# A listed order for an attention phase, and the first expert chosen 384 tokens earlier

## The chip, the cores and the metric

One core of one Trainium2 chip. TensorE (PE; PEld is its weight load), VectorE (DVE), ScalarE (ACT), GpSimd (POOL) and SyncE (SP) each work through a list of instructions of their own, in order, and wait for each other by semaphores. The metric is the device time of one launch in microseconds. All data are float32 in HBM; matmuls run in float32, each as two instructions of the trace.

## What is computed

Two blocks follow each other. The first is a gated linear recurrence with complex gates per batch (4), head (8) and channel (48) over 768 time steps:

```python
for t in range(S):
    new_re = ar * S_re - ai * S_im          # gates, limited in magnitude
    new_im = ar * S_im + ai * S_re
    S_re, S_im = new_re + k[t] (x) v[t], new_im
    y[t] = q[t] @ S_re
```

Its output, laid out as 3072 tokens of 384 numbers, goes into a top-1 mixture of 8 experts:

```python
expert_idx = argmax(x @ w_gate)
gate_w     = softmax(x @ w_gate)[expert_idx]
out[mask]  = gate_w[mask] * (relu(x[mask] @ w1[e]) @ w2[e])     # 384 -> 1024 -> 384
```

## The kernel before

**Attention** is worked in chunks of 128 time steps, 6 to a batch, 24 in all. The gates become logarithms and angles, whose running sums (DVE scans) turn the recurrence into masked matmuls: within a chunk scores times values, between chunks a state of 96x48 per head.

- `front(u)` prepares one *unit* of 128, 256 or 384 time steps. There are ten: units 0 to 2 are batch 0, 3 and 4 batch 1, 5 and 6 batch 2, and 7 (384 steps), 8 (256) and 9 (128) batch 3. It loads gates and q, k (L335), runs logarithms, exponentials and sines on ACT with changes of the function table, scans (L357, L368) and elementwise work on DVE, and two multiplications per unit on POOL. It ends with four products on DVE into `zp` (L388) and ten DMAs on SP (L398, L401) that move `zp` into `hz0` or `hz1`, the layout in which PE reads it.
- `chunk(b, c)` is PE's part: transposed keys (L431), scores (L438), which DVE masks into `am` (L442), the state's and the values' share of the output (L450, L457), the new state (L465), and a transposing matmul (L473) whose result ACT copies into `xg` (L476). The logits come out of that same matmul.
- `route(b, r0, r1)` sorts tokens into experts: some 15 small DVE instructions, a count on PE (L514 to L519), and one indirect DMA per chunk on POOL (L533) that puts the rows into `xs_hbm`, 480 places for each expert. Batches 0 to 2 are routed whole, batch 3 after its chunks 2, 4 and 5. `cum` holds the places taken so far, `cumb` its bf16 copy for PE.
- `ranks()` (L540) runs once, when 2688 tokens are routed: it sorts the experts by their counts into `order`.
- `early_rows()` (L558) then lets SP read the number of the fullest expert from `order` (L256), load the two halves of its w1 (L573) and, once those 2688 tokens are in `xs_hbm`, its first 320 rows (`EARLY = 10` blocks of 32, L567), and its w2 (L575). w1 and w2 go into the two halves of `hz0`, which batch 3's first half has left.
- `early_layer()` (L582) is the first layer of that expert for those 320 rows, 24 matmuls on PE (L590), before the last tokens are routed.

**The experts** follow in turns, turn 0 being the fullest. `tokens(e)` loads rows (L736) and lets DVE transpose them (L260), `weights(e)` loads w1 and w2 (L726), then come the first layer (L767), the second (L786) and the scatter to the output (L707). Turn 0 has only its remaining 160 rows to load and to compute. The three w1 buffers are `hz0`, `hz1` and one of its own.

What sets the order: every step is entered into a `Plan` with an engine, a planned duration and the keys that it reads and writes. `Plan.order()` (L151) tries 144 priority rules in a list scheduling on these planned durations, and the steps are written to the engines in the order that comes out shortest. `P.PE` (L285) scales PE's planned durations. The expert phase has a second `Plan`, `M`.

Of the kernel before, what the change touches and what calls it, by code (L numbers as in the profile page):

```python
# [10 lines left out]
FP32 = mybir.dt.float32  # L11
BF16 = mybir.dt.bfloat16
I32 = mybir.dt.int32
# [7 lines left out]
C = S // 128  # L21
# [17 lines left out]
EARLY = 10  # L39
# [9 lines left out]
BIG = 1e9  # L49


class Plan:
# [27 lines left out]
    PE = 1.0, 1.0, 0.0  # L80
# [20 lines left out]
    def run(self, prio, edges, ins, back, stick):  # L101
# [10 lines left out]
        for _ in ops:  # L112
# [23 lines left out]
            free[eng] = issued = end = t + o["dur"] * (self.PE[t > self.PE[2] or back] if eng == "PE" else 1.0)  # L136
# [32 lines left out]
def gateloop_then_moe(ctx, tc, gates, qk, v, wg, w1, w2, out):  # L169
# [57 lines left out]
    key, above = const([128, E], "key"), const([128, E], "above")  # L227
# [3 lines left out]
    cum = const([128, E], "cum")  # L231
    cumb = const([128, E], "cumb", dt=BF16)
    nc.vector.tensor_scalar_mul(cum, base, 1.0 / 128)
    nc.vector.tensor_copy(cumb, cum)
# [9 lines left out]
    w1b, w2b = [z[:, 0:DT * F] for z in hz], [z[:, DT * F:2 * DT * F] for z in hz]  # L244
# [10 lines left out]
    def expert_of(e, eng):  # L255
        return ds(nc.values_load(order[0:1, TURNS[e]:TURNS[e] + 1], engines=(eng,), min_val=0, max_val=E - 1,  # L256
                                 skip_runtime_bounds_check_because="experts have numbers below E"), 1)
# [5 lines left out]
    with ExitStack() as att:  # L263
# [21 lines left out]
        P.PE = 1.8, 1.12, 60.0  # L285
# [192 lines left out]
        def route(b, r0, r1):  # L478
# [50 lines left out]
            dv(0.2, lambda: tt(cum, cum, ohs, ALU.add), ("ohs", "cum"), ("cum",))  # L529
            dv(0.2, lambda: nc.vector.tensor_copy(cumb, cum), ("cum",), ("cumb",))  # L530
# [8 lines left out]

        def ranks():  # L540
# [6 lines left out]
            dv(lambda: tt(key, cnt, keyb, ALU.subtract), ("RT",), ("key",))  # L547
            dv(lambda: tt(tmp, bc(key[:, None, :], full), bc(key[:, :, None], full), ALU.is_le), ("key",), ("tmp",))
# [9 lines left out]
        def early_rows():  # L558

            P.add("free", 0.0, lambda: None, (), tuple(("h", 0, c, h, part, d0) for c in range(3) for h in range(H) for part in range(2)  # L560
                                                       for d0 in (0, 32)) + ("hz0",))
            P.add("free", 0.0, lambda: None, (), (("A", 0), ("B", 0), "xb0"))
            P.add("free", 0.0, lambda: None, (), (("Q", 0), ("K", 0), "xrt0"))
            P.add("free", 0.0, lambda: None, (), tuple(("zp", part, x) for part in range(2) for x in range(2)) + ("ht0",))
            P.add("SP", 0.5, lambda: which.update({0: expert_of(0, mybir.EngineType.SP)}), ("order",), (("which", 0),))
            for i in range(4):
                last = P.add("SP", 0.65, lambda i=i: nc.sync.dma_start(  # L567
                    xb[0][32 * i:32 * i + 32, None, 0:EARLY, :], xv[:, which[0], 0:EARLY, 104 * i:104 * i + 96]),
                    (("which", 0), "xb0") + tuple(("rows", B - 1, c) for c in range(3)), (("xbA", i),), lat=2.0, wire=0.8)
# [389 lines left out]
```

## Time and profile before

| | us |
|---|---|
| three runs | 528.9, 529.66 (median), 532.79 |
| the profiled execution's own time | 530.8 |
| its span, first to last instruction | 529.0 |
| last transposing matmul of attention (L473) ends | 245.85 |
| first layer of the early rows (L590) | 249.17 to 265.4 |
| PE's last matmul ends | 522.8 |

| engine | busy us | share | instructions |
|---|---|---|---|
| PE | 450.7 | 85% | 2738 |
| DVE | 266.4 | 50% | 433 |
| ACT | 206.0 | 39% | 299 |
| POOL | 115.1 | 22% | 125 |

A share over the whole span hides that there are two phases. Until about 224 us DVE is the busy engine, with PE close behind from 60 us on; from 265 us on PE alone is. ACT loads its function table 25 times, 1283 ns each (L642).

### The profile page before, as it was taken

How to read it: one execution, taken by the hardware profiler on the slowest of the kernel's cores; microseconds unless marked ns; L12 is line 12 of the kernel's file. 1: busy time of each engine (PE TensorE's matmuls, PEld its weight loads, DVE VectorE, ACT ScalarE, POOL GpSimd, SP SyncE). 2: the span in 40 equal slices, each digit the busy share in tenths (PEclk: the TensorE clock that was granted, in tenths of full speed). 3: DMA queues.
4: the chain of work that ended last, by engine and by line, in shares of the span. 5: the costliest groups of instructions: out<-in, count | busy, mean ns of one | idle time of the engine just before them, and what ended most of it. 6: DMA issues, size and time to landing. Idle time of an engine off the chain costs nothing. (4 is left out here: it accounts for less than half of the span.)

```text
span 529.0 us, 7236 instructions
## 1 busy us (share of the span) xinstructions
PE 450.7 (85%) x2738; PEld 319.0 (60%) x2738; DVE 266.4 (50%) x433; ACT 206.0 (39%) x299; POOL 115.1 (22%) x125
## 2 busy tenths in 40 slices
PE   0055788898797398896999999999999999999995
PEld 0045677797697398885667554555555555555552
DVE  6899999999889899844001410122211111201101
ACT  6996887998595877442201000001000010010000
POOL 6174122142604621251000101010110202000012
PEclk9999789899979599998999999999999999999999
DMA  8577496786997974358597780304920451000001
GB/s 265 174 241 222 130 308 165 240 225 219 271 313 181 254 212 108 107 167 283 135 339 213 218 265 30 135 15 142 307 65 9 156 225 48 0 30 14 16 27 44
DMA packets 47945, 86.19 MB, mean 163 GB/s; under 512 B 21136, under 2 KB 36779, under 8 KB 45984
## 3 DMA queue, kind: packets, MB, share of 16 engines
q1 hardware_dynamic: 44064, 75.44, 47.9%
q0 software_dynamic: 3200, 9.86, 5.1%
q8 instruction: 23, 0.38, 0.3%
q10 hardware_dynamic: 640, 0.37, 0.3%
q14 instruction: 18, 0.15, 0.1%
HBM read 53.93 MB, written 13.24 MB: 127 GB/s over the span
## 5 line engine op out<-in xcount | busy, mean ns | idle before, releaser
L438 PE MATMUL bank<-hz 128*128 128x128 f32 x384 | 62.8, 321 | 42.9 <-DMA hz<-zp 31.1
L767 PE MATMUL bank<-Z,hz 128*128 128x416 f32 (+2 forms) x288 | 90.9, 468 | 0.0
L438 PEld LDWEIGHTS bank<-hz 128*128 128x128 f32 x384 | 56.1, 228 | 47.2 <-DVE cs L368 27.7
L707 POOL DMA_INDIRECT out_dram<-yo,gi x24 | 23.5, 977 | 243.2 <-DVE yo L718 229.5
L767 PEld LDWEIGHTS bank<-Z,hz 128*128 128x128 f32 x288 | 52.1, 190 | 35.4 <-issue 20.3
L773 ACT ACTIVATE ht<-bank 128x416 f32<-128x416 f32 (+2 forms) x20 | 10.1, 511 | 154.8 <-PE bank L767 154.8
L718 DVE TENSOR_SCALAR yo<-bank,gi 128x384 f32<-128x384 f32 x24 | 14.7, 616 | 92.5 <-PE bank L786 92.5
L786 PE MATMUL bank<-hz,ht 128*128 128x384 f32 (+1 forms) x176 | 59.5, 487 | 0.0
L182 DVE TENSOR_TENSOR zp<-Z,cs 128x1152 f32<-128x1152 f32 (+2 forms) x40 | 45.8, 1189 | 2.1 <-ACT cs L302 1.6
L786 PEld LDWEIGHTS bank<-hz,ht 128*128 128x128 f32 (+1 forms) x176 | 30.5, 175 | 19.9 <-issue 2.4
L770 DVE TENSOR_SCALAR ht<-bank 128x416 f32<-128x416 f32 (+2 forms) x20 | 11.6, 582 | 58.9 <-PE bank L767 58.9
L182 POOL TENSOR_TENSOR AB<-AB,C 128x1152 f32<-128x1152 f32 (+2 forms) x9 | 22.6, 2513 | 70.5 <-ACT C L302 64.6
L786 PE MATMUL bank<-w2b,ht 128*128 128x384 f32 (+1 forms) x128 | 37.5, 487 | 0.0
L786 PE MATMUL bank<-w2b,zp 128*128 128x384 f32 (+1 forms) x112 | 37.5, 486 | 0.0
L533 POOL DMA_INDIRECT xs_hbm<-xg,slot x24 | 27.2, 1134 | 42.7 <-DVE am L182 18.9
L767 PE MATMUL bank<-Z,w1b 128*128 128x448 f32 (+1 forms) x96 | 36.1, 517 | 0.0
L431 PE MATMUL bank<-ident,hz 96*128 96x96 f32 x160 | 22.4, 275 | 16.0 <-DMA hz<-zp 14.4
L465 PE MATMUL bank<-v,kt 128*96 128x48 f32 x320 | 31.9, 253 | 4.1 <-ACT kt L433 4.1
L773 ACT ACTIVATE zp<-bank 128x160 f32<-128x160 f32 (+2 forms) x12 | 5.2, 437 | 76.9 <-PE bank L767 62.0
L182 DVE TENSOR_TENSOR am<-bank,causal 128x512 f32<-128x512 f32 x48 | 31.7, 680 | 5.7 <-PE bank L438 3.9
L465 PEld LDWEIGHTS bank<-v,kt 128*96 128x96 f32 x320 | 30.3, 170 | 5.7 <-ACT kt L433 4.4
L182 POOL TENSOR_TENSOR Z<-Z,AB 128x1152 f32<-128x1152 f32 (+2 forms) x9 | 22.0, 2442 | 51.3 <-ACT AB L302 51.3
(135 smaller groups left out, 681.1 us busy)
## 6 DMA issues: line engine op xcount, KB each, us to landing
hz<-in_w_dram SPq DMA_DIRECT2D x9, 1536.0 KB
hz<-zp SPq DMA_DIRECT2D x24, 432.0 KB, 5.7
AB<-in_gates_dram SPq DMA_DIRECT2D x12, 576.0 KB, 3.8
Z<-in_qk_dram SPq DMA_DIRECT2D x12, 576.0 KB, 5.1
w2b<-in_w_dram SPq DMA_DIRECT2D x4, 1536.0 KB
v<-in_v_dram SPq DMA_DIRECT2D x8, 576.0 KB, 7.1
w1b<-in_w_dram SPq DMA_DIRECT2D x2, 1536.0 KB, 9.3
hz<-zp SPq DMA_DIRECT2D x8, 288.0 KB, 4.7
```

What stands on the lines that cost most here:

```text
L182: (eng or nc.vector).tensor_tensor(out=o, in0=a, in1=b, op=op)
L431: nc.tensor.transpose(KT[hf][:, (h % 4) * 96:(h % 4) * 96 + 96], hk[0:96, h], ident[0:96, 0:96])
L438: nc.tensor.matmul(SC[hf][:, (h % 4) * 128:(h % 4) * 128 + 128], lhsT=hk[:, h], rhs=hq[:, h], start=True, stop=True)
L465: nc.tensor.matmul(ST[0:96, h * D:h * D + D], lhsT=kt[par][:, h * 96:h * 96 + 96], rhs=V[:, cl, h * D:h * D + D], start=(c == 0 and h == 0 ...
L533: i = nc.gpsimd.indirect_dma_start(out=xs_hbm[:, :], out_offset=bass.IndirectOffsetOnAxis(ap=R[slot][:, c:c + 1], axis=0), in_=xg[:, (g0 + ...
L707: i = nc.gpsimd.indirect_dma_start(out=out[:, :], out_offset=bass.IndirectOffsetOnAxis(ap=index, axis=0), in_=y, in_offset=None, bounds_ch ...
L718: M.add("DVE", 0.62, lambda: nc.vector.tensor_scalar_mul(yo[yi], OB[ob][:, 0:DM], gate), (("O", ob),) + reads, (("yo", yi),))
L767: nc.tensor.matmul(HB[hb][:, 0:n - n0], lhsT=w1b[e % NW][:, c:c + 128], rhs=xrt[s][:, d, n0:n], start=(d == 0), stop=(d == DT - 1))
L770: M.add("DVE", 0.6, lambda f_=f_, hb=hb: nc.vector.tensor_scalar_max(ht[h][:, f_, n0:n], HB[hb][:, 0:n - n0], 0.0), (("H", hb),), (("ht", ...
L773: M.add("ACT", 0.6, lambda f_=f_, hb=hb: nc.scalar.activation(ht[h][:, f_, n0:n], HB[hb][:, 0:n - n0], func=ACT.Relu), (("H", hb),), (("ht ...
L786: nc.tensor.matmul(OB[ob][p0:p0 + m, 0:DM], lhsT=ht[t % NH][:, f_, c0:c0 + m], rhs=w2b[t % NV][:, f_ * DM:f_ * DM + DM], start=(f_ == 0), ...
```

## The change

1. **The order is listed.** `ORDER`, 989 numbers, says in which order attention's steps are written to the engines, in place of `P.order()`. The expert phase keeps its planner. The planner's model of PE's speed gets a third level, which no longer matters for attention's order.

```diff
+ORDER = [int(i) for i in (
+    "0 1 62 3 63 4 64 5 65 6 2 7 46 8 297 9 187 66 10 67 11 68 21 12 13 69 24 70 23 15 83 14 16 22 26 143 25 27 28 18 17 19 71 20 142 72 30 29 34 31 33 32 "
...
+).split()]
-        P.PE = 1.8, 1.12, 60.0
+        P.PE = (0.0, 1.8), (60.0, 1.12), (180.0, 0.95)
-            for i in P.order():
+            assert sorted(ORDER) == list(range(len(P.ops)))
+            for i in ORDER:
```

2. **The first expert is chosen at 2304 tokens**, when batch 2 is routed, by a function of its own. `ranks()` stays at 2688 tokens for the other seven; it puts the chosen one in front by adding `far`.

```diff
+        def fullest():
+            cnt = bank[2][:, 440:440 + E]
+            P.add("PE", 0.3, lambda: nc.tensor.matmul(cnt, lhsT=ones_b, rhs=cumb, start=True, stop=True), ("cumb",), ("RT",))
...
+            dv(lambda: tt(key, cnt, keyb, ALU.subtract), ("RT",), ("key",))
+            dv(lambda: nc.vector.tensor_reduce(top, key, axis=AX, op=ALU.max), ("key",), ("top",))
+            dv(lambda: nc.vector.scalar_tensor_tensor(out=above, in0=key, scalar=top, in1=e_f, op0=ALU.is_equal, op1=ALU.mult), ("top",), ("above",))
...
+                    nc.vector.tensor_reduce(first, above, axis=AX, op=ALU.add)
...
+            dv(lambda: nc.vector.tensor_scalar(out=far, in0=key, scalar1=top, scalar2=FAR, op0=ALU.is_equal, op1=ALU.mult), ("top", "key"), ("far",))
         def ranks():
...
+            dv(lambda: tt(key, key, far, ALU.add), ("far",), ("key",))
```

3. **The early rows** are 288 (`EARLY = 9`), they are loaded once batch 2's tokens are in `xs_hbm`, and w1 is loaded in one DMA into a buffer of its own, `w1first`, which needs no space that attention uses. w2 still goes into `hz0`. The three w1 buffers of the expert phase become `w1first`, `hz0`, `hz1`, and the one that the expert phase had of its own is gone.

```diff
-EARLY = 10
+EARLY = 9
-    w1b, w2b = [z[:, 0:DT * F] for z in hz], [z[:, DT * F:2 * DT * F] for z in hz]
+    w1b, w2b = [keep.tile([128, DT * F], FP32, name="w1first")] + [z[:, 0:DT * F] for z in hz], [z[:, DT * F:2 * DT * F] for z in hz]
-            P.add("SP", 0.5, lambda: which.update({0: expert_of(0, mybir.EngineType.SP)}), ("order",), (("which", 0),))
+            P.add("SP", 0.5, lambda: which.update({0: expert_of(0, mybir.EngineType.SP)}), ("first",), (("which", 0),))
...
-                    (("which", 0), "xb0") + tuple(("rows", B - 1, c) for c in range(3)), (("xbA", i),), lat=2.0, wire=0.8)
+                    (("which", 0), "xb0") + tuple(("rows", B - 2, c) for c in range(C)), (("xbA", i),), lat=2.0, wire=0.8)
+            P.add("SP", 0.65, lambda: nc.sync.dma_start(w1b[0][:, None, :], w1v[:, which[0], :]), (("which", 0),), (("w1", 0),), lat=1.9, wire=5.2)
...
-                bk, key = ((bank[7], "ones"), (bank[3], ("KT", 1)), (bank[5], "ST"))[f_ % 3]
+                bk, key = ((bank[7], "ones"), (bank[3], ("KT", 1)), (bank[5], "ST"))[(0, 0, 0, 1, 2, 0, 1, 2)[f_]]
...
-        w1b += buf("w1b", NW - 2, [128, DT * F])
```

4. **The places taken** are summed in bf16 directly: `cum` and its six casts into `cumb` (L530) are gone.

```diff
-            dv(0.2, lambda: tt(cum, cum, ohs, ALU.add), ("ohs", "cum"), ("cum",))
-            dv(0.2, lambda: nc.vector.tensor_copy(cumb, cum), ("cum",), ("cumb",))
+            dv(0.2, lambda: tt(cumb, cumb, ohs, ALU.add), ("ohs",), ("cumb",))
```

Where the listed order puts things, by the engines' lists of the built program. ACT still loads its table 25 times. On DVE, 16 instructions that stood ahead of unit 6's last product now stand behind it: four masks of batch 2, one scan of unit 7 and 11 small ones of batch 1's routing. Seven of unit 5's (six scans and an L355) now stand ahead of unit 4's last product; ahead of the last products of units 7, 8 and 9 stands almost the same as before. On PE, one transposing matmul (L473) more stands behind the first use of unit 7. The early layer's 24 matmuls are still PE's last of the phase, behind the last transposing matmul, and the last routing count stands behind six of them rather than three. On SP, reading `first`, loading w1 and loading w2 now stand ahead of the ten moves of unit 9; the early rows' four loads stand behind these ten. On POOL, all six of batch 3's scatters now wait for these four loads, where three did.

## Prediction

> **What bounds it now.** The chain of waits is of no use here: it holds four pieces and reaches back only to 5.4 us before the span's end. So I read the stretches first: busy time of each engine (with instructions) between marks of the timeline, then granted clock, DMA share, GB/s.
>
> ```profile
> core 0: us, PE busy (x) PEld busy (x) DVE busy (x) ACT busy (x) POOL busy (x), PEclk, DMA share, GB/s
> ...
> 172.00:180.20 8.20, 0.04 (x1) 0.07 (x2) 8.10 (x13) 6.53 (x8) 3.99 (x3) 0.50 1.02 214
> 180.20:200.40 20.20, 20.20 (x209) 18.96 (x209) 17.81 (x26) 16.61 (x27) 8.02 (x8) 0.88 0.78 236
> 200.40:246.00 45.60, 41.63 (x465) 37.74 (x463) 31.26 (x90) 23.97 (x44) 11.99 (x14) 1.00 0.49 145
> 246.00:258.90 12.90, 8.96 (x27) 5.73 (x27) 3.23 (x17) 1.91 (x5) 3.15 (x4) 0.74 0.54 185
> 258.90:265.40 6.50, 6.50 (x24) 4.64 (x25) 0.74 (x2) 1.75 (x4) 0.00 (x0) 1.00 0.99 228
> 265.40:522.90 257.50, 257.41 (x900) 146.57 (x898) 44.83 (x92) 15.80 (x33) 23.91 (x25) 1.00 0.36 115
> ```
>
> From 265.4 on PE never rests: what is saved before it moves the end one for one, and what PE gains in work there costs in full. From 200.4 to 246 PE is busy 41.6 of 45.6 us. Before that PE stands still for 8 us while DVE is full. The timeline at the marks (start, length, engine, line; in brackets the idle time before and what ended it):
>
> ```profile
> 180.16 0.88 PE L431 MATMUL bank<-ident,hz 96*128 96x96 f32 x4 [10.93 <-DMA hz<-zp]
> ...
> 200.39 0.97 PEld L438 LDWEIGHTS bank<-hz 128*128 128x128 f32 x8 [0.19 <-DMA hz<-zp]
> ...
> 244.71 1.14 PE L473 MATMUL bank<-turn,yt 128*128 128x104 f32 x8 [0.74 <-ACT yt L461]
> ...
> 247.77 1.30 DVE L260 STREAM_TRANSPOSE Z<-AB 128x384 f32<-128x384 f32 x3 [0.95 <-DMA AB<-xs_hbm]
> ...
> 249.17 3.54 PE L590 MATMUL bank<-Z,hz 128*128 128x320 f32 x6 [3.33 <-issue]
> ...
> 258.87 6.73 PE L590 MATMUL bank<-Z,hz 128*128 128x320 f32 x24 [0.77 <-ACT zp L592]
> ...
> 265.44 10.48 PE L786 MATMUL bank<-hz,zp 128*128 128x384 f32 x32
> 275.76 6.68 PE L767 MATMUL bank<-Z,hz 128*128 128x160 f32 x48
> ```
>
> PE waits 10.9 us for unit 6, then works through batch 2's last three chunks and meets unit 7 (200.39) when it has just landed. Attention ends at T = 244.71 + 1.14 = 245.85. Then PE waits 3.3 us for the early rows, which DVE transposes only at 247.77, and the first six matmuls take 590 ns each where the last 24 take 280.
>
> **The seam.** Before, 265.44 - 245.85 = 19.6 us lie between attention's last transposing matmul and the second layer. After, w1 and the early rows depend on batch 2 alone, so the 3.3 us should go, and with no hole the clock should stay up: 48 instructions at 280 x 288/320 = 252 ns are 12.1 us, with the routing count 0.2 makes 12.3. Turn 0 then has 192 columns left instead of 160: 6.68 us x 192/160 = 8.0, 1.3 more. Gain 19.6 - 12.3 - 1.3 = **6.0**. It holds 3.3 of waiting, 2.1 of cold matmuls (16.3 - 48 x 0.28 = 2.9, less 0.8 waiting for a bank at 258.87) and that 0.8; that the bank wait goes too is the new bank pattern. Bounds: 0 to 6.2.
> The cold part can be read in two ways. The clock was 0.58 from 246 to 250, 0.57 to 254 and 1.00 after: about five of PE's microseconds at half speed. The Trainium skill (TensorE: Matmul & The Clock Gate, What's actually happening) has it that the clock halves after an idle window of about 3.4 us and returns after a busy window as long. By that rule the loss is an estimated 1.7 us and the seam gives 5.6; it also speaks against the change, since any new hole of that length brings the cold stretch back. The sum goes by the row.
>
> What hides the rest of the seam: turn 0's last rows came to 262.03 (DVE's transposes end), T + 16.2, and are needed at T + 12.3 + 10.5 = T + 22.8. Turn 1's w1, now into `hz0`, can be asked for at about the same place as before and takes 9.3 us to land; it is needed after 8.0 us more, T + 30.8. Both cost nothing; without that cover w1 would cost its 9.3.
>
> **Small edits.** Six casts (L530) go, mean 482 ns; `fullest` and `far` add six DVE instructions of about 0.2 us, as the rows of `ranks` (0.15 to 0.22). Neither is on PE's path; 0. `fullest`'s count is one matmul of 0.17, and one L473 group (1.06) more stands behind unit 7: **+1.2** in the stretch that PE fills. The waits of batch 3's scatters for the early rows cost six times 1.28 (0.98 and 0.30 of issue) on POOL at most; five of them end before the last one's slot is known, 8.7 us after T (254.53). 0.
>
> **The listed order.** Nothing is removed, so a gain can only come from idle and stretched time.
> PE between 200.4 and T: 4.0 idle. I take half, **-2.0** (bounds 0 and -4.0).
> The landing of unit 7: DVE's work ahead of its last product is nearly the same, so it moves only by DVE's idle and stretched time. DVE waited four times for PE's scores between 155 and 186 (0.78 + 0.97 + 0.80 + 0.84 = 3.4), two of them with PE cold behind the 10.9 us hole. Four masks and 12 other instructions (4 x 0.68 + 0.99 + 11 x 0.2 = 5.9 us) now come after unit 6's products, so unit 6 should land about 6 us sooner, with PE still having those chunks to do: the hole shrinks to some 5 us or less, and these waits go: **-3.4**. The hole itself gives nothing, since PE would then wait at unit 7. In exchange unit 4 lands later by seven instructions, six scans at 0.99 and one at 0.75 = 6.7 us; the 10.9 us of slack at unit 6 take that up.
> What I can't price is how DVE's instructions meet POOL's:
>
> ```profile
> 157.93 3.33 POOL L182 TENSOR_TENSOR Z<-Z,AB 128x1152 f32<-128x1152 f32 x1 [16.30 <-ACT AB L302]
> 158.81 3.67 DVE L182 TENSOR_TENSOR zp<-Z,cs 128x1152 f32<-128x1152 f32 x1
> ```
>
> The product, 1.32 when alone (two in 2.63 us at 164.24), takes 3.67: it ends 1.2 us after POOL's multiplication does. Over the groups: 18 scans L357 at 1387 ns against 990 alone (7.1), 24 products at 1483 against 1315 (4.0), 12 of L351 and L374 at 1808 and 1742 against 1350 (5.1), four of L373 and L376 at 1496 and 1602 against 680 (3.5), the six casts (1.9): 21.6 us of DVE's time is stretch. POOL's 18 multiplications last 44.6 us, so 23.0 now lie beside something that they don't hold up. Half of either is my bound, -10.8 to +11.5. I take 0: the order around each multiplication is new, and no row says which way.
>
> Sum: -6.0 + 1.2 - 2.0 - 3.4 = -10.2. The profiled execution's own time is 530.8 (1.8 around its span), so 520.6; the median lies 1.1 below that execution: 519.5, **520**.
>
> **Rivals.**
> (a) *The stretch falls too.* Half of it gone from DVE's path moves unit 7's landing by 10.8: 519.5 - 10.8 = 509. For it: DVE is full up to 224 us. Against: 45 us of PE's work stand behind the landing anyway, and PE was only just idle at 200.4.
> (b) *A transfer comes in the way at the seam.* On SP the loads of w1 and w2 now stand ahead of unit 9's moves, and w2 waits for PE's last read of `hz0`. From that read PE has 18.9 us to go to unit 9's first scores (3 score groups of 1.1, 6 of L457 at 0.62, 3 of L465 at 1.5, 3 of L473 at 1.06, 3 of L431 at 0.5, 2 of L450 at 1.08, 0.4 of counts). w2 needs 9.3 (w1b's row of the same size) and the moves 5.3: 14.6, a margin of 4.3. If both loads are in front, 18.6 + 5.3 = 23.9, PE waits 5.0 and runs cold for 2.1: 519.5 + 7.1 = 527. The early rows follow the moves, 2.0 of issue and 2.8 of landing: with one load in front they are there 5.5 us before T.
> The Trainium skill (DMA: Bandwidth & Descriptors, Queues, rings and completion order) says that each DMA engine takes a queue's descriptors in ring order, which is the case against this change; no run here shows yet what it costs.
> (c) *Slower: the new order meets POOL's multiplications worse.* Half of the 23.0 covered microseconds become stretch ahead of unit 7's products, and the gains of the order fall out: 530.8 - 6.0 + 1.2 + 11.5 - 1.1 = 536. It ends slower than before once the new stretch exceeds 4.8. For it: L351, L355, L373 and the products stand in other places around all 18; against: 21.6 of 44.6 are already stretched, so the old order was no good cover either.
>
> **How the numbers follow.** Forecast (514 to 525) 0.48, (a) 0.17, (b) 0.20, (c) 0.15. Faster by over 1% (what a measurement of this kernel can tell from no change) is under 524.4: the forecast but for 0.02, (a), and 0.03 of (b), 0.66. Within 1% up to 535: 0.02, the other 0.17 of (b) and 0.02 of (c), 0.21. Slower 0.13. Range 509 to 533: half of (a) lies below, most of (c) above.
>
> **What would show it.** The seam: L590's matmuls (then of 288 columns) begin within 1 us of the last L473 and take 12 to 13 us together, and L786 begins 12 to 13.5 us after it. The order: T between 239 and 245; PE's wait for unit 6 under 6 us; the four score waits gone; DVE's group means for (a) below, for (c) above those quoted. For (b): an idle PE before unit 9's first scores, ended by DMA. I am wrong if T comes later than 248, or if the early layer waits for rows.

## The result and the profile after

Over 20 runs of each kernel the median is 529.21 us after and 529.78 before: 0.998 of the time before, 95% interval 0.996 to 1.001. That is no change that can be measured. Medians here and below are of all runs; ratios and intervals leave out the runs that fell into a slower state of the chip (one of after's 20). The profiled execution took 527.76 (span 526.1, mean clock 0.972), against 530.8 (529.0, 0.959) before.

The span falls into three pieces, and each can be held against the prediction: T, the end of attention's last transposing matmul; the seam from there to the first matmul of the second layer; and the rest.

| span, us | before | predicted | after |
|---|---|---|---|
| T | 245.85 | 241.65 | 247.81 |
| seam | 19.6 | 12.3 | 14.6 |
| from there to the end | 263.6 | 264.9 | 263.7 |
| sum | 529.0 | 518.8 | 526.1 |

So the seam gave 5.0, T gave 2.0 back, and the ten microseconds became three; the medians show less than one.

**The seam.** The timeline of after there (start, length, engine, line; in brackets the idle time before and what ended it). Lines of the file are some 30 to 50 higher than before: L504 is the transposing matmul, L636 the early layer, L638 its relus on ACT, L787 the loads of turn 0's remaining rows, L837 the second layer, L563 the scatters.

```profile
246.67 1.14 PE L504 MATMUL bank<-turn,yt 128*128 128x104 f32 x8 [0.74 <-ACT yt L492]
247.64 3.10 PE L636 MATMUL bank<-Z,w1first 128*128 128x288 f32 x12
...
252.37 0.41 ACT L638 ACTIVATE zp<-bank 128x288 f32<-128x288 f32 x1 [1.18 <-PE bank L636]
255.19 2.24 ACTq L787 DMA_DIRECT2D AB<-xs_hbm  x1
257.47 0.41 ACT L638 ACTIVATE zp<-bank 128x288 f32<-128x288 f32 x1 [4.69 <-issue]
...
251.99 0.98 POOL L563 DMA_INDIRECT xs_hbm<-xg,slot  x1 [0.69 <-POOL xg L535]
...
257.94 4.63 PE L636 MATMUL bank<-Z,w1first 128*128 128x288 f32 x18 [2.69 <-ACT zp L638]
262.40 9.84 PE L837 MATMUL bank<-hz,zp 128*128 128x384 f32 x30
```

The early layer starts at once, as forecast, and its clock stays at 1.00. But PE then waits 2.69 us for a relu that ACT could have done nearly four microseconds sooner: its six matmuls, the seventh to twelfth of those from 250.63 on, end at about 253.7 by their spacing. ACT's list has, between the third relu (252.37) and the fourth (257.47), the issue of a load of turn 0's remaining rows, and that load may only start when the last scatter of batch 3 (POOL, 251.99 + 0.98) has landed; the issue then begins at 255.19 and takes 2.24 us. The profile calls these 4.69 us "issue", since ACT's queue itself is what waits.

**Attention.** Busy time between marks, with matmuls counted (x), granted clock, DMA share and GB/s: first of after, then of before.

```profile
core 0: us, PE busy (x) PEld busy (x) DVE busy (x) ACT busy (x) POOL busy (x), PEclk, DMA share, GB/s
...
100.00:150.00 50.00, 39.64 (x397) 35.37 (x397) 48.48 (x58) 41.19 (x55) 12.11 (x5) 0.93 0.77 212
150.00:180.00 30.00, 25.69 (x289) 23.07 (x285) 26.67 (x42) 26.92 (x38) 12.12 (x8) 1.00 0.89 218
180.00:200.00 20.00, 18.98 (x158) 17.64 (x159) 13.15 (x20) 10.61 (x17) 6.28 (x8) 0.74 0.98 279
200.00:240.00 40.00, 37.82 (x439) 35.04 (x438) 29.89 (x77) 25.40 (x46) 12.10 (x14) 1.00 0.69 218
```

```profile
100.00:150.00 50.00, 44.12 (x479) 40.33 (x474) 47.65 (x62) 41.77 (x57) 17.60 (x10) 0.94 0.79 232
150.00:180.00 30.00, 19.23 (x220) 17.94 (x218) 27.43 (x40) 21.64 (x32) 10.34 (x5) 0.84 0.88 225
180.00:200.00 20.00, 19.84 (x204) 18.82 (x206) 17.61 (x24) 16.41 (x27) 7.67 (x9) 0.87 0.78 238
```

Added up from the start of the span, PE has done 837 matmuls of attention at 150 us after the change and 909 before, 1126 and 1129 at 180, 1284 and 1333 at 200 (a matmul that crosses a mark counts in both stretches). The 10.9 us hole before unit 6 is gone and yet nothing is won by 180: before, PE stood still because it had run 72 matmuls ahead, and unit 6 lands no sooner now: PE's wait for it ends at 180.33, before at 180.16. Behind 180 the changed kernel falls back by 46. There DVE has least to do (13.15 of 20 us), while the DMA engines are full (0.98). The timeline of after shows what they carry:

```profile
159.87 2.84 SPq L429 DMA_DIRECT2D hz<-zp  x3
165.38 0.67 SPq L676 DMA_DIRECT2D xs_hbm<-empty  x1
166.14 10.51 SPq L429 DMA_DIRECT2D hz<-zp  x7
...
177.32 1.32 SPq L676 DMA_DIRECT2D xs_hbm<-empty  x2
...
181.64 2.63 DVE L213 TENSOR_TENSOR zp<-Z,cs 128x1152 f32<-128x1152 f32 x2 [3.79 <-DMA hz<-zp]
...
189.56 0.69 DVE L213 TENSOR_TENSOR am<-bank,causal 128x512 f32<-128x512 f32 x1 [4.28 <-PE bank L469]
...
180.33 0.46 PE L469 MATMUL bank<-hz 128*128 128x128 f32 x2 [2.74 <-DMA hz<-zp]
```

and the same moves before:

```profile
166.89 9.62 SPq L398 DMA_DIRECT2D hz<-zp  x10
```

`xs_hbm<-empty` are three DMAs that fill the unused places with empty rows, 64, 64 and 96 places for each of 8 experts: by 418 floats a row 836, 836 and 1254 KB. Before, they were issued from 147.0 to 148.1, ahead of unit 6's moves and with nothing urgent behind them. In the listed order the first stands between the third and the fourth of unit 6's ten moves. It is issued 4.7 us after the last of six scatters has ended on POOL (159.72 + 0.97), which write the same buffer, so seven moves stand behind a wait for those scatters; then they are issued at 1.5 us each instead of 0.96. The other two fills follow at 177.3. Unit 6's products end 8.3 us sooner on DVE than before (161.7 against 170.0), but its last move is issued at 176.65, as before (176.51).

### The profile page after: what moved, and what is told of

Same layout as the page of the kernel before. It is cut to its first block, busy times and chain, and to the rows that moved or that the text cites. A ratio compares the mean times of both kernels' runs of the same rounds, so it can differ in the third digit from the quotient of the medians.

```text
span 526.1 us, 7224 instructions
## 1 busy us (share of the span) xinstructions
PE 451.0 (86%) x2739; PEld 321.3 (61%) x2739; DVE 263.2 (50%) x432; ACT 206.2 (39%) x299; POOL 111.7 (21%) x125
## 5 line engine op out<-in xcount | busy, mean ns | idle before, releaser
L818 PE MATMUL bank<-Z,hz 128*128 128x416 f32 (+2 forms) x240 | 84.4, 507 | 0.0
L818 PEld LDWEIGHTS bank<-Z,hz 128*128 128x128 f32 x240 | 45.5, 190 | 36.1 <-issue 22.0
L837 PE MATMUL bank<-hz,ht 128*128 128x384 f32 (+1 forms) x176 | 59.3, 488 | 0.0
L769 DVE TENSOR_SCALAR yo<-bank,gi 128x384 f32<-128x384 f32 x24 | 14.7, 617 | 80.2 <-PE bank L837 74.1
L213 DVE TENSOR_TENSOR zp<-Z,cs 128x1152 f32<-128x1152 f32 (+2 forms) x40 | 42.6, 1111 | 7.4 <-DMA hz<-zp 3.8
L837 PEld LDWEIGHTS bank<-hz,ht 128*128 128x128 f32 (+1 forms) x176 | 30.3, 175 | 20.4 <-issue 2.9
L818 PE MATMUL bank<-Z,w1first 128*128 128x192 f32 (+2 forms) x144 | 41.0, 441 | 0.0
L462 PEld LDWEIGHTS bank<-ident,hz 96*128 96x128 f32 x160 | 17.2, 154 | 38.3 <-issue 33.6
L213 POOL TENSOR_TENSOR AB<-AB,C 128x1152 f32<-128x1152 f32 (+2 forms) x9 | 21.4, 2377 | 78.7 <-ACT C L333 43.7
L496 PE MATMUL bank<-v,kt 128*96 128x48 f32 x320 | 33.1, 260 | 5.6 <-ACT kt L464 5.6
L837 PE MATMUL bank<-w2b,ht 128*128 128x384 f32 (+1 forms) x128 | 37.6, 488 | 0.0
L837 PE MATMUL bank<-w2b,zp 128*128 128x384 f32 (+1 forms) x112 | 37.4, 486 | 0.0
L818 PEld LDWEIGHTS bank<-Z,w1first 128*128 128x128 f32 x144 | 26.1, 190 | 14.5 <-issue 7.3
L824 ACT ACTIVATE zp<-bank 128x192 f32<-128x192 f32 (+2 forms) x12 | 5.4, 446 | 72.7 <-PE bank L818 72.7
```

What stands on the lines that cost most here:

```text
L213: (eng or nc.vector).tensor_tensor(out=o, in0=a, in1=b, op=op)
L462: nc.tensor.transpose(KT[hf][:, (h % 4) * 96:(h % 4) * 96 + 96], hk[0:96, h], ident[0:96, 0:96])
L496: nc.tensor.matmul(ST[0:96, h * D:h * D + D], lhsT=kt[par][:, h * 96:h * 96 + 96], rhs=V[:, cl, h * D:h * D + D], start=(c == 0 and h == 0 ...
L769: M.add("DVE", 0.62, lambda: nc.vector.tensor_scalar_mul(yo[yi], OB[ob][:, 0:DM], gate), (("O", ob),) + reads, (("yo", yi),))
L818: nc.tensor.matmul(HB[hb][:, 0:n - n0], lhsT=w1b[e % NW][:, c:c + 128], rhs=xrt[s][:, d, n0:n], start=(d == 0), stop=(d == DT - 1))
L824: M.add("ACT", 0.6, lambda f_=f_, hb=hb: nc.scalar.activation(ht[h][:, f_, n0:n], HB[hb][:, 0:n - n0], func=ACT.Relu), (("H", hb),), (("ht ...
```

## The experiments

Ratios are to the kernel before in the same runs, with 95% intervals. That kernel's median was 529.2 to 530.5 on four chips and 535.5 on one, which served the first four experiments, so across sets ratios are compared, not times. Where an edit is a list of numbers, its diff shows pieces of the list or says it in words.

### First set: the two halves, and the two waits seen

**order_only**: before, with attention's steps in the listed order and the rest of the change left out (early choice, 288 rows, `w1first`, no casts).

```diff
-            for i in P.order():
+            for i in ORDER:     # the listed order, in the numbers of before's steps
```

> The kernel before, with every operation of attention in the listed order on its engine, and nothing else of the change: the first expert is still chosen at the end, and the early rows, the loads and the early layer stand as before. Theory A (the order gives nothing, the seam gave the little that there is): attention ends where it does in the changed kernel, 247.8 us less the 1.2 of the group and count that only the early choice brings, so 246 to 248 against 245.85, and the seam is the old 19.6 us: ratio to before 1.000 to 1.006. Theory B (the order gains what the prediction had it gain, 4.2 to 5.4 us, and the early choice took it back through its extra transfers and waits): attention ends at 240 to 242, ratio 0.990 to 0.993.

546.04, ratio 1.018 (1.013 to 1.023). The timeline of this kernel:

```profile
250.05 0.22 DVE L584 TENSOR_REDUCE order<-tmp 128x8 int32<-128x64 f32 x1
...
263.22 1.30 DVE L289 STREAM_TRANSPOSE Z<-AB 128x384 f32<-128x384 f32 x3 [10.55 <-DMA AB<-xs_hbm]
...
264.62 3.54 PE L619 MATMUL bank<-Z,hz 128*128 128x320 f32 x6 [12.93 <-DVE sub L211]
```

T is 251.70, later than either theory had it. The list was made for a kernel in which nothing hangs on `ranks()`. Here the early rows do, and it writes their choice at 250.05, so PE waits 12.9 us. The run tells what the list costs without the early choice, not what the list is worth.

**early_only**: after, with attention's steps in the order that before's planner had found, and the new steps put in by hand.

```diff
-ORDER = the listed order
+ORDER = before's own order, fullest() and early_rows() put in where their data are ready
```

> The changed kernel with attention's operations put back, engine by engine, into the order that the kernel before has; the early choice, its loads and the layer of 288 columns stay. Theory A: attention ends near 246 to 247 (245.85 and the count), the seam takes 14.6 us as in the changed kernel's trace against 19.6, the rest 1.3 longer: 3 to 4 us shorter than before, ratio 0.992 to 0.995, so faster than the whole change. Theory B (it is the early choice that costs): no faster than the whole change, 0.998 or more.

540.4, ratio 1.004 (1.000 to 1.009). These places were ill chosen: a count stood ahead of PE's scores (2.42 us of waiting, for `cumb`), and DVE waited 3.78 us for early rows with two masks queued behind, which cost PE 3.65. So neither half is measured by this set; the fourth does it again.

**rest_on_sp**: after, with all four loads of turn 0's remaining rows on SP.

```diff
-            if e == 0:
-                M.add("ACT", 0.5, lambda: which.update({"ACT": expert_of(0, mybir.EngineType.Activation)}), (), (("which", "ACT"),))
...
-                eng, dma, wh = ("ACT", nc.scalar, "ACT") if e == 0 and i % 2 else ("SP", nc.sync, e)
+                eng, dma, wh = "SP", nc.sync, e
```

> The changed kernel with the two quarters of turn 0's last rows that ACT's queue issues given to SP's. Theory A (the 2.69 us that PE waits inside the early layer come from this: the loads wait for the last scatters, and the early layer's later results wait behind them on ACT): the wait goes, the second layer begins 12 to 12.5 us after attention's last matmul in place of 14.6, the time falls by 2 to 2.7 us against the whole change, ratio to before 0.993 to 0.995. Rival (the wait is for the banks of PSUM whatever ACT's queue holds, or SP's longer queue delays turn 1 by as much): within 0.5 us of the whole change, 0.998.

528.99, ratio 0.986 (0.982 to 0.991). The wait inside the early layer is gone and the seam is 11.9 us; the relus follow each other as PE fills the banks.

**empties_early**: after, with the three fills moved ahead, to 52, 75 and 101 us. The steps of the list are numbers; 298 to 300 are the fills.

```diff
-... 425 694 298 720 ... 437 436 299 546 ... 682 700 300 520 ...
+... 169 348 300 55 ... 358 461 298 220 ... 307 506 299 375 ...
```

> The changed kernel with its three fills of empty rows (836, 836 and 1254 KB; they stand between and behind the moves of unit 6 in the listed order, at 165 and 177 us) put into three stretches in which the DMA engines rest: at 52, 75.6 and 100 us. Theory A (in the changed kernel they slow unit 6's moves: 1.5 us each against 0.96 before): unit 6 lands 2 to 4 us sooner, PE's two waits for it (2.74 and 0.69 us) and DVE's 3.79 shrink, and the clock of 0.60 from 180 to 190 us, where PE does 58 matmuls and not some 110, comes back: 3 to 6 us off, ratio to before 0.987 to 0.993. Rival (PE is behind for other reasons, and the fills then hold up units 2 to 4): 0.998 or above.

531.39, ratio 0.990 (0.985 to 0.995). Unit 6's ten moves are together again (163.44, 9.21 us) and DVE's 3.79 wait is gone. But the fill at 101 us now stands among moves and gate loads of units 3 to 5: PE waits 1.85 at 98.09 and 2.42 at 101.22 for `hz`. T stays late, 248.96, and the seam is 18.4 us in this trace: PE's wait inside the early layer is 3.58 us, and its last 18 matmuls take 7.38 us (4.63 in after) at a granted clock of 0.50 from 260 to 264.

### Second set: after once more, and better places for the fills

**whole_again**: after, unchanged.

> The changed kernel once more, every engine's operations in the same order, beside the variants of it that run on the same chip. It gives the figure that these are to be read against: the kernel before took 529.8 us on one chip and 535.5 us on another, so a ratio from one chip says little of a difference of 2 us on the other. If the 1.4% that the rest rows on SP's queue showed is that edit's own 2.7 us (0.5%) and a chip that suits the changed kernel better than the old one, this run stands at 0.990 to 0.993; if the edit alone is worth 7 us, at 0.998.

529.44, ratio 0.998 (0.995 to 1.001). T = 247.63, seam 15.1. The same end came about in another way. In this kernel's timeline the seven moves behind the first fill are slow again, but PE loses only 1.2 us to them; the two later fills do the harm:

```profile
164.05 0.67 SPq L675 DMA_DIRECT2D xs_hbm<-empty  x1
164.81 10.78 SPq L428 DMA_DIRECT2D hz<-zp  x7
...
176.27 1.32 SPq L675 DMA_DIRECT2D xs_hbm<-empty  x2
...
184.28 2.09 SPq L365 DMA_DIRECT2D AB<-in_gates_dram  x1
...
196.75 0.52 ACT L332 ACTIVATE AB<-AB 128x384 f32<-128x384 f32 x1 [4.62 <-DMA AB<-in_gates_dram]
...
200.75 0.46 ACT L499 COPY sb<-bank 96x384 f32<-96x384 f32 x1
...
201.26 1.95 PE L480 MATMUL bank<-hz,sb 128*48 128x128 f32 x16 [4.86 <-ACT sb L499]
```

Unit 9's gates, asked for at 184.28, are there only at 196.7. ACT waits 4.62 us for them, with the copy of the state (`sb`) queued behind, and PE waits 4.86 us for that copy. In the first trace of after PE was later by then, and the same gates cost nothing more.

**rest_fills**: rest rows on SP, and the fills at 52 (1254 KB), 75 and 113 us; the last one behind unit 4's first five moves.

```diff
-... 425 694 298 720 ... 437 436 299 546 ... 682 700 300 520 ...
+... 169 348 300 55 ... 358 461 298 220 ... 312 559 384 299 476 ...
```

> The changed kernel with the rest rows on SP's queue and the three fills of empty rows moved: 1254 KB at 52 us, 836 KB at 75.6 us, 836 KB at 113 us behind the first five moves of unit 4 (at 100 us it had held up the gates of a later unit). Theory A (the fills at 165 and 177 us cost the changed kernel what the order gained at unit 6): unit 6's ten moves are issued within 9.5 us from 160 us on, so that it lands 6 to 7 us sooner than 181 us, DVE does not wait 3.8 us for zp, attention ends 2 to 4 us sooner than with the rest rows alone; ratio to the whole change 0.988 to 0.992. Rival (PE is behind its own work from 100 us on and does not meet unit 6's landing any more): attention ends within 1 us of where it did, ratio to the whole change 0.994 to 0.996, from the rest rows alone.

521.06, ratio 0.983 (0.977 to 0.989). T = 244.09, seam 11.6. **rest_fills_again**, the same edits in a later set:

> The version with the rest rows on SP's queue and the fills at 52, 75.6 and 113 us once more, on the chip of the kernel above, to narrow its interval (0.977 to 0.989 in five runs) and to set the listed order against the old one: 0.980 to 0.986 if the parts add up as the single edits showed them, 0.987 or above if the first figure was a lucky one. Against the early choice in the old order it should be 0.4 to 0.8% shorter by theory A, and the same by the rival that the listed order is worth nothing even without the fills.

521.02, ratio 0.984 (0.979 to 0.989). T = 242.95, seam 11.64. Its timeline at the places of the last two fences:

```profile
158.05 11.43 SPq L428 DMA_DIRECT2D hz<-zp  x10
...
192.51 0.52 ACT L332 ACTIVATE AB<-AB 128x384 f32<-128x384 f32 x1
...
197.32 1.08 PE L480 MATMUL bank<-hz,sb 128*48 128x128 f32 x16 [0.56 <-ACT sb L499]
```

ACT takes unit 9's gates 4.2 us sooner and no longer waits for them, and PE gets the state 3.9 us sooner. The DMA share from 180 to 200 us is 0.63 instead of 0.98 to 1.02. The seam of the first of the two traces:

```profile
242.95 1.14 PE L503 MATMUL bank<-turn,yt 128*128 128x104 f32 x8 [0.74 <-ACT yt L491]
243.93 3.10 PE L635 MATMUL bank<-Z,w1first 128*128 128x288 f32 x12
...
246.91 8.98 PE L635 MATMUL bank<-Z,w1first 128*128 128x288 f32 x36
255.72 6.61 PE L834 MATMUL bank<-hz,zp 128*128 128x384 f32 x20
```

**rest_unit4**: rest rows on SP, and unit 5's seven DVE instructions back behind unit 4's last product. The rival was that unit 4's late landing costs PE its lead.

```diff
-... 229 484 385 306 314 383 473 558 386 320 474 387 312 559 384 476 321 475 313 336 ...
+... 229 385 306 314 383 558 386 320 387 312 559 384 321 ... 328 319 381 484 473 474 476 475 479 478 337 ...
```

> The changed kernel with the rest rows on SP's queue and, in the listed order, unit 5's six scans and its clamp (6.7 us of DVE's work that stand ahead of unit 4's last product) put behind that product, and the load of a later unit's gates behind unit 4's moves. Theory A (the order lost at unit 4 what it gained at unit 6: at 150 us PE has done 853 of its matmuls in the changed kernel and 924 in the kernel before, because unit 4 lands 7 us later): unit 4's last moves are issued near 113 us in place of 120, PE has done 20 to 60 matmuls more at 150 us, attention ends 2 to 5 us sooner; ratio to the whole change 0.986 to 0.992. Rival (DVE's order is what counts, and unit 5's work, now 2 us later, brings every later landing 2 us later): attention ends at the same time or up to 2 us later, ratio to the whole change 0.995 to 1.000.

527.75, ratio 0.993 (0.990 to 0.997). Unit 4's moves are all issued by 118.5 instead of 125.3, but PE then waits for transposed keys, which ACT copies:

```profile
121.71 2.63 PE L495 MATMUL bank<-v,kt 128*96 128x48 f32 x15 [4.23 <-ACT kt L463]
```

PE has done 828 matmuls at 150 us, no more than in the two traces of after (837 and 847), and T is 249.26. So an earlier landing of unit 4 alone mends nothing; the new wait for keys may hide what it is worth.

### Third set: each repair alone, and the fills in the kernel before

**rest_alone** is the edit of rest_on_sp, on another chip.

> The changed kernel with the rest rows on SP's queue and nothing else, beside the fills alone on one chip. Theory A: this removes the 2.7 to 3.2 us that PE waits inside the early layer and no more: ratio to before 0.991 to 0.993 where the whole change stood at 0.998. Rival (the 0.986 that the edit showed on an earlier chip is its size everywhere): 0.984 to 0.988.

524.29, ratio 0.990 (0.986 to 0.994). Seam 11.6, T = 247.55, and the wait for `sb` is there as in whole_again (5.42 us).

**fills_alone** moves the fills as in rest_fills and leaves the rest rows on ACT.

> The changed kernel with its three fills of empty rows at 52, 75.6 and 113 us, the rest rows left on ACT's queue. Theory A: attention ends near 244 us in place of 247.6, the early layer keeps its wait of about 3 us and the seam its 14.6 to 15.1: 3.5 us less than the whole change, ratio to before 0.990 to 0.993; with the rest rows' 0.5% that adds up to the 0.983 of both together. Rival (the two only work together, since the wait inside the early layer grows when attention ends sooner: the last scatters still come when they came): the wait grows to 4 us or more and the ratio is 0.994 to 0.998.

526.19, ratio 0.990 (0.986 to 0.994). The profiled execution was its longest (528.75, where others took 521.8 to 528.3), and its T of 248.46 shows no gain; its seam is 14.7, with a wait of 2.77. So the gain of the fills alone stands on the times, not on this trace.

Together the four kernels make a square: 0.998 for neither repair, 0.990 for either, 0.983 and 0.984 for both. The two add up.

**before_fills**: before, with its fills issued at 51.9, 73.7 and 75.6 us instead of from 147 on, and the order of all else kept.

```diff
-            for i in P.order():
+            for i in ORDER:     # before's own order; the three fills ahead
```

> The kernel before, every engine's order as it was but for the three fills, which go to 51.8, 74.2 and 96.4 us from 147 us. It asks whether the listed order was needed at all. Theory A (in the kernel before unit 6 is late because DVE makes its products late, and PE, ahead of DVE, then waits 10.9 us; the fills at 147 us stand ahead of unit 6's moves and not among them): unit 6 lands within 1 us of where it did, no gain, ratio 0.997 to 1.002. Rival (the fills cost the old order as much as the new one): 3 us or more off, ratio 0.990 to 0.994.

532.44, ratio 1.004 (1.001 to 1.006). PE waits 4.1 us for `hz` at 96 us, where the kernel before waits 2.7 at 94.6, and the hole at unit 6 stays, shorter but ending 3.3 us later. T is 249.40 in this trace, the longest of its executions (535.35):

```profile
95.97 0.90 PE L460 MATMUL bank<-ident,hz 96*128 96x96 f32 x4 [4.09 <-DMA hz<-zp]
...
183.45 0.87 PE L460 MATMUL bank<-ident,hz 96*128 96x96 f32 x4 [8.86 <-DMA hz<-zp]
```

Early fills are thus no gain in themselves. In the changed kernel they mend what its own order did to them.

### Fourth set: what the listed order is worth

**early_old_order**: everything of the change except the listed order, with the new steps in better places than in early_only: the count one group later on PE, the choice behind the masks on DVE, both weight loads behind unit 9's moves, the early rows' transposes late. Rest rows on SP.

```diff
-ORDER = the listed order
+ORDER = before's own order, the new steps placed as said
...
-                eng, dma, wh = ("ACT", nc.scalar, "ACT") if e == 0 and i % 2 else ("SP", nc.sync, e)
+                eng, dma, wh = "SP", nc.sync, e
```

> The early choice without the listed order, put together with more care than the first attempt (there the choice's count stood ahead of PE's scores, the first weights between unit 9's moves, and the early rows' transposes ahead of two masks on DVE). Attention's operations stand in the order of the kernel before; the count comes one group later on PE, the choice on DVE behind the masks, both loads behind unit 9's moves, the transposes behind the last route but one; the rest rows are issued by SP. Theory A (the parts add up, and the listed order is worth some 3 us once the fills are out of its way): attention ends near 247 us (245.85 and 1.2 for the group and the count), the seam takes 11.6 to 12.0, the rest 1.3 more: 525.4 for an execution like the profiled one, ratio to before 0.987 to 0.992, between the whole change and the version with rest rows and fills. Theory B (the old order has no room for the early choice: what it moves holds up unit 9 or the masks): attention ends at 250 us or later, ratio 0.995 or above.

520.69, ratio 0.984 (0.979 to 0.988), the same as rest_fills_again beside it. Its timeline:

```profile
177.25 0.87 PE L461 MATMUL bank<-ident,hz 96*128 96x96 f32 x4 [8.57 <-DMA hz<-zp]
...
241.43 1.14 PE L503 MATMUL bank<-turn,yt 128*128 128x104 f32 x8 [0.74 <-ACT yt L491]
...
254.20 2.10 PE L834 MATMUL bank<-hz,zp 128*128 128x384 f32 x6
```

The hole at unit 6 is still 8.6 us long, but it ends at 177.25 and not at 180.16, and T is 242.57 and not 245.85. The two go together in all traces of before's order (early_only, with its extra waits behind, left out):

| kernel | wait for unit 6 | ends at | T | between | matmuls in between |
|---|---|---|---|---|---|
| early_old_order | 8.57 | 177.25 | 242.57 | 65.32 | 673 |
| early_old_act | 8.10 | 177.36 | 243.06 | 65.70 | 673 |
| before | 10.93 | 180.16 | 245.85 | 65.69 | 671 |
| before_again | 11.36 | 180.37 | 245.84 | 65.47 | 671 |
| before_no_cast | 11.11 | 182.07 | 247.23 | 65.16 | 671 |
| before_fills | 8.86 | 183.45 | 249.40 | 65.95 | 671 |

PE is busy for 61.6 to 62.5 us of each of these stretches. So the length of the hole says how far PE had run ahead, and T moves with its end. In after the wait for unit 6 ends at 180.33, with 675 matmuls and 67.5 us to T.

What the listed order gains with its fills and rows repaired, before's own order has as well.

**early_old_act**: the same with half of the rest rows on ACT, as in the change.

```diff
-                eng, dma, wh = "SP", nc.sync, e
+                eng, dma, wh = ("ACT", nc.scalar, "ACT") if e == 0 and i % 2 else ("SP", nc.sync, e)
```

> The early choice in the old order, as in the version with 520.7 us, but with half of the rest rows left on ACT's queue as the change has them. Theory A (the early layer's wait comes from these loads and belongs to the early choice, whichever order attention has): a wait of 2.2 to 3.3 us inside the early layer, the seam at 14.6 to 15.2 in place of 11.6, attention's end unchanged near 242.6: 3 to 3.5 us more than with SP, ratio to before 0.988 to 0.992; so the early choice alone would have been a gain of about 1%, and the listed order is what took it back. Rival (the wait was one of the listed order's, or attention's early end was the SP edit's): ratio below 0.986 or above 0.995.

524.77, ratio 0.990 (0.986 to 0.994). T = 243.06, seam 14.0. The profile names here what it called "issue" in after:

```profile
251.63 0.43 ACTq L786 DMA_DIRECT2D AB<-xs_hbm  x1
252.11 0.41 ACT L637 ACTIVATE zp<-bank 128x288 f32<-128x288 f32 x1 [4.08 <-DMA xs_hbm<-xg,slot]
...
252.58 4.63 PE L635 MATMUL bank<-Z,w1first 128*128 128x288 f32 x18 [2.08 <-ACT zp L637]
```

ACT waits for a scatter's landing (`xs_hbm<-xg,slot`). This kernel is the whole change without the listed order. It is 1.05% faster than before where the change is 0.2%, so the listed order took most of the early choice's gain back (the intervals, 0.986 to 0.994 and 0.996 to 1.001, lie apart).

**before_no_cast**: before, with the six casts gone and `cumb` summed directly.

```diff
-            dv(0.2, lambda: tt(cum, cum, ohs, ALU.add), ("ohs", "cum"), ("cum",))
-            dv(0.2, lambda: nc.vector.tensor_copy(cumb, cum), ("cum",), ("cumb",))
+            dv(0.2, lambda: None, ("ohs", "cum"), ("cum",))
+            dv(0.2, lambda: tt(cumb, cumb, ohs, ALU.add), ("cum", "ohs"), ("cumb",))
```

> The kernel before without the six copies of the running counts into bf16: the counts are added up in bf16 at the place of the copy, and the separate additions go (thirteen small DVE instructions become six or seven). Order, moves and layers are as before. Theory A (with the early choice in the old order attention ended at 242.6 us, 3.3 sooner than before although 1.2 us more work stands behind unit 7: the copies, of which one takes 2.06 us beside a multiplication of POOL's ahead of unit 7's products, were on DVE's path): 2 to 4 us less, ratio 0.992 to 0.996. Theory B (the prediction: they are on nobody's path): 0.998 to 1.002, and the 3.3 us are the difference of two executions.

528.85, ratio 0.998 (0.995 to 1.001): no change that can be told from none. T is 247.23 in its trace, the longest of its executions (532.74).

**before_again**: before, unchanged, for a second trace.

> The kernel before once more, its order unchanged, for a second and independent trace. With the early choice in the old order attention ended at 242.6 and 243.1 us in two executions; in the one profiled execution of the kernel before it ended at 245.85, and the copies account for 0 to 3 us of time by their interval (0.9945 to 1.0005). Theory A (the early choice or the missing copies moved attention's end): it ends within 1 us of 245.85 again, and unit 6 ends PE's wait at 180 us. Theory B (attention's end scatters by as much from execution to execution): it ends 1.5 us or more away from 245.85, with the wait for unit 6 ending as much sooner or later.

530.28, ratio 1.001 (0.998 to 1.004). T is 245.84 (245.85 in the first trace), with a wait of 11.36 for unit 6. So theory A's mark came. But the two traces are of executions of nearly the same time (530.8 and 530.58), where before's runs range from 527.9 to 533.2: they don't show how far T moves from run to run. In the listed order the same edits gave 244.09 and 242.95 (rest_fills), 250.32 and 247.55 (rest_on_sp and rest_alone, the first on the slower chip).

## Why the prediction was wrong

520 was forecast and 529.2 measured. The range of 509 to 533 held it; the likeliest case did not come.

| kernel, us of span | T | seam | rest | sum |
|---|---|---|---|---|
| after | 247.81 | 14.6 | 263.7 | 526.1 |
| after again | 247.63 | 15.1 | 263.8 | 526.6 |
| rest_fills | 244.09 | 11.6 | 263.7 | 519.4 |
| early_old_act | 243.06 | 14.0 | 263.6 | 520.7 |
| early_old_order | 242.57 | 11.6 | 263.6 | 517.8 |

- **"Unit 6 should land about 6 us sooner"** is the step that failed. The move on DVE was right and larger than forecast (8.3 us), but the landing also needs SP, and there I read only the queue around unit 9. The fills, three large DMAs that the list carried from 147 us in among unit 6's moves and ahead of unit 9's gate load, were in no term. Unit 6's last move was issued at 176.65 (176.51 before), and the wait for it ended at 180.33 (180.16): it landed no sooner. Rest_fills differs from rest_alone by their place alone: its T is 3.5 us earlier (4.6 in the second trace).
- **"The hole itself gives nothing, since PE would then wait at unit 7"** is right of the hole's length and wrong of its end. The length was PE's lead: in after it is gone because PE had done 72 matmuls fewer at 150 us. Its end counts: in the six traces of before's order T follows it at 65.16 to 65.95 us. In early_old_order PE met unit 7 at 198.43, after a wait of 0.17 (200.39 and 0.19 before), so unit 7 came sooner too. Its T is 1.5 us ahead of rest_fills' first trace and 0.4 ahead of its second.
- **-3.4 for four score waits and -2.0 for half of PE's idle time**: in after, two DVE waits of 3.79 and 4.28 stand in the place of the four, and PE's idle time from 200.4 to T fell from 3.8 to 2.9. Of the four, the two behind the hole (0.80 and 0.84) are gone in early_old_order, in before's own order. No run shows a gain of the listed order: with its faults mended it equals the old order (0.984 and 0.984), and as written it costs 0.9% (0.990 for early_old_act against 0.998), or 4.8 us of T.
- **The seam, 12.3**: right in mechanism, 11.6 where ACT is free. The early layer started within 0.2 us of T and took 12.2 us of PE's time, with no cold part. The row had been weighed against the rule of the Trainium skill (TensorE: Matmul & The Clock Gate, What's actually happening) that an idle window of about 3.4 us halves the clock. The wait of 3.33 before left the clock at 0.58; those of 2.69, 2.08 and 2.21 in after, early_old_act and early_only left it at 1.00. That is near the page's figure; closer to it the runs don't agree on the wait alone (last section). What the term missed is ACT's queue: 3.0 us in after, 3.5 between whole_again and rest_alone, 2.4 between the last two rows of the table. The sign of it stood in the trace of before. The 0.77 us in front of the early layer's last 24 matmuls, which the prediction put down to the pattern of banks, is the same wait, as ACT's timeline there shows:

```profile
257.69 0.64 ACTq L736 DMA_DIRECT2D AB<-xs_hbm  x1
258.38 0.44 ACT L592 ACTIVATE zp<-bank 128x320 f32<-128x320 f32 x1 [3.04 <-PE bank L590]
```

  The relu at 258.38, for which PE waited, stands behind a load of rest rows that the last scatter (254.53 + 0.99) let go at 257.69. Counted from T, PE needed this relu at 12.3 us before and its counterpart at 7.4 after; ACT got past the load at 12.5 before and only at 9.7 after. So the wait grew from 0.77 to 2.69.
- **+1.3 for 192 columns**: the group is dearer as worked out (8.1 us against 6.7), but the rest of the span is as long as before. From the second layer on PE is busy 258.4 us against 257.4, so 1.0 of the 1.3 came; behind its last matmul follow 5.3 us against 6.2. Why that end is shorter is not shown.
- **Unit 4 later by 6.7, taken up by slack**: 7.4 later. No run shows a cost: rest_unit4 took it back and gained nothing, but met a wait for ACT's keys instead.
- **Small edits 0**: before_no_cast does not speak against it; its interval leaves room for up to 0.5%.
- **The rivals.** (a) and (c) turned on DVE's stretch beside POOL. It fell a little: the 128x1152 products average 1349 ns against 1483, and DVE's whole busy time 263.2 us against 266.4, nothing near the 10.8 us of (a). (b) had the right kind of cause, a transfer ahead of moves on SP, in the wrong place: it named w1 and w2 at unit 9, which PE never waited for (its items for PE add up to 18.8 us, not 18.9, and its 5.3 for the ten moves is the landing of one: after issued the ten in 9.30), and it was the fills at unit 6 and behind.

Two of the marks set for being wrong decide it: T was to come between 239 and 245 and came at 247.8, just under the 248 that was named; and PE's wait for unit 6 fell to 2.74 as claimed without T following.

**What stays open.** Early_old_order's T is 3.3 us before that of the kernel before, in the same order of attention's steps. The wait for unit 6 ends 2.9 us sooner, and with it T; but unit 6's moves begin only 0.8 us sooner, and why the landing quickens is not shown. Why PE has fewer matmuls done at 150 us in the listed order isn't shown either; putting unit 4 back did not mend it.

Both early_old_order (520.69) and rest_fills (521.06 and 521.02) are 1.6 to 1.7% faster than the kernel before, which the change itself is not.

## What to carry to other kernels

When an order is moved, follow every queue through it, DMA issues with no urgent reader included: a large fill that nobody waits for can delay the moves and loads that everybody waits for. A DMA issued from a computing engine's queue holds that engine for as long as the DMA's own wait lasts (ACT stood idle for 4.69 us in after), so put loads that wait for late data on a queue with nothing urgent behind them. The length of an idle stretch says how far that engine ran ahead; what counts is when the stretch ends and how much work stands behind it. Count the instructions done at fixed marks, before and after, to tell the two apart.

## What the hardware showed

**A DVE instruction of a few columns can take 2 us beside a multiplication on POOL.** The timeline of before, and then of after, around one multiplication on POOL:

```profile
176.06 2.62 POOL L182 TENSOR_TENSOR Z<-Z,AB 128x1152 f32<-128x1152 f32 x1 [7.26 <-ACT AB L302]
...
176.59 0.14 DVE L339 COPY lend<-D 128x9 f32<-128x9 f32 x1
176.65 2.06 DVE L530 CAST cumb<-cum 128x8 bf16<-128x8 f32 x1
```

```profile
147.11 2.62 POOL L213 TENSOR_TENSOR Z<-Z,AB 128x1152 f32<-128x1152 f32 x1 [6.95 <-ACT AB L333]
...
147.21 2.55 DVE L213 TENSOR_TENSOR cumb<-cumb,ohs 128x8 bf16<-128x8 bf16 x1
```

Both end when POOL's multiplication ends (178.71 and 178.68; 149.76 and 149.73). The same bf16 addition takes 0.17 at 176.39 in after, with POOL idle. A bf16 result is not needed for it: in before a float32 subtraction of 48 columns takes 1.85 at 113.36, beside POOL's multiplication from 111.99 to 115.13, and 0.21 at 152.96; in after a float32 copy of 6 columns takes 1.85 at 200.31, when a multiplication of 1.82 starts on POOL. Others pass: the copy of 9 columns above takes 0.14. The Trainium skill (SBUF — State Buffer, Who interferes with whom) speaks of an exclusive lock on ports that DVE and GpSimd share; these rows agree with it; which instructions are held is not worked out here. It also explains why dropping the casts saved little: in before_no_cast the addition that is left takes 2.07 at that place.

**The clock fell after shorter waits, too.** In the trace of after, PE's waits of 2.74 and 0.69 us, which end at 180.3 and 181.7, are followed by a granted clock of 0.60 from 180 to 190, where PE did 58 matmuls (94 in whole_again, where the waits there are 0.94 and 0.26). Nor is the length of one wait enough near 3.4 us: behind 3.24 in whole_again the clock was 1.00, behind 3.20 in before_again 0.54 from 246 to 250, behind 3.58 in empties_early 0.50.
